# A transformer block, forward and backward: another order of all 1972 operations, other buffer homes, and one store that waits for a transpose

## The chip, the cores and the metric

The kernel runs on one core of a Trainium2 chip. The core has five engines, each with an instruction stream of its own: TensorE (PE, matrix multiplication; PEld is its loading of weights), VectorE (DVE), ScalarE (ACT), GpSimd (POOL) and SyncE (SP, which here only issues DMAs). They synchronise by semaphores. Operands lie in the SBUF (128 partitions), sums in the eight banks of the PSUM, and everything else in DRAM, from where and to where 16 DMA engines carry it. The metric is the time of one execution on the device in microseconds (us), the median of the runs; lower is better.

## What is computed

One block with pre-layer-norm, 2048 positions of 512 numbers in bfloat16: attention with 32 heads of 16, in which a position sees itself and seven earlier ones, two apart (a sliding window, dilated), and a dense pair of layers, 512 to 1792 to 512, with GELU between. The outputs are the block's result and its gradients for x and the weights and biases.

```
def _A_ref(x, wqkv, wo):
    ...
    off = jnp.arange(W) * dil            # W, dil = 8, 2
    idx = pos[:, None] - off[None, :]
    ...
    logits = jnp.einsum("bhsd,bhswd->bhsw", q, kg) * scale
    attn = _softmax(jnp.where(mask, logits, -1e9), axis=-1)
    o = jnp.einsum("bhsw,bhswd->bhsd", attn, vg)
    return merge_heads(o) @ wo

h  = x + _A_ref(_layernorm(x), A_wqkv, A_wo)
h2 = h + _B_ref(_layernorm(h), B_w1, B_b1, B_w2, B_b2)
...
_out, _vjp = jax.vjp(_f, A_x, A_wqkv, A_wo, B_w1, B_b1, B_w2, B_b2)
return (_out, *_vjp(grad_out))
```

(The lines are shortened; `merge_heads` stands for a transpose and a reshape.)

## The kernel before

The sequence is cut into four chunks of 512 rows, each of four tiles of 128 rows. The work of a chunk is written as stages, each a function that records operations: `p1_ln` to `p1_h` for the forward attention, `p2_h`, `p2_out`, `p2_dg` and `p2_bwd` for the dense layers and their backward pass, `p3_go` to `p3_gl1` for the backward pass of the attention, and `wg_ffn` for the gradients of the weights. An operation is a group of instructions on one engine with the buffers that it reads and writes. Nothing is issued while it is recorded. At the end of the function

```
    pl.emit(ORDER, HOMES)
```

issues all 1972 of them. `ORDER` is a table of their numbers: it sets the order of the program, and so the order on each engine and each queue. `HOMES` gives each buffer its place, in units of 64 bytes in the SBUF or as a PSUM bank. Two buffers may have the same place one after the other; the later one's writer then waits for the readers of the earlier one. `emit` requires that each operation stands behind those it depends on.

The table also decides a form of instruction. `mmul` (L268 and L270) writes a product with 128 weight columns either as one matmul (L270) or as four with 32 columns each (L268): the second form is taken in runs that stand between two operations which need 32 columns anyway (the sums L487 and L527).

What the steps of the prediction touch, in the order of a chunk's way through the kernel:

- `consts` and `warm` (L307 to L350) set constants at the start: `ident` by POOL, S (`S4`) by DVE from `ident`, `wz` by DVE, a block of zeros for fill matmuls on PE (L311).
- `layernorm` (L353 on): statistics st and mv by DVE (L360, L361), `ve` by DVE (L371), its power -1/2 `rstd` by POOL (L373), `nm` by DVE (L376), the scaled rows by ACT.
- `p1_attn`: the products `prf` of queries and shifted keys on DVE (L479), their sums on PE (L487), the largest `mx` on DVE (L690), its subtraction on PE (L270).
- `p1_o`: POOL gathers the neighbouring rows of v into R (L471, 2304 KB); DVE multiplies them with the coefficients to `prbo` (L518), four products for a chunk; PE sums each (L527); ACT puts the sum into `ost` (L532). Chunks 1 and 3 then get `ost` with rows and columns exchanged, `oT`, by a DMA transpose of SP (L291); the other two get it by PE. POOL stores `ost` to DRAM (L287, 512 KB) for the gradient of wo.
- `p1_h`: PE multiplies `oT` with wo, DVE adds x to h (L747), and the second layer norm follows.
- `p2_h`, `p2_dg`, `p2_bwd`: matmuls on PE with `w`, `w1T`, `w2T`, `goT` (transposed by SP, L291), evictions xb by ACT (L774), GELU gl by ACT (L777), its derivative by DVE and ACT (L792 to L803), gradients by DVE (L856), the layer norm backward (L561 to L570), which ends in `ghr`.
- `p3_go`: `ghT`, the transpose of `ghr` by SP (L291), times wo gives `got`, evicted by ACT (L297). `p3_dots` and `p3_bands` repeat the attention's kinds of products with the gathers Rq, Rk, Rv.
- `wg_ffn`: products over all rows for the gradients of the weights, evicted by ACT or DVE (L297) and stored (L287); the last are those of wqkv (`wgsq`).

The function that this change extends takes the buffers which an operation waits for as `r=`; so far a store waits for its source alone:

Of the kernel before, what the change touches and what calls it, by code (L numbers as in the profile page):

```python
# [159 lines left out]
def kernel(  # L160
# [30 lines left out]
    NC = S // CH  # L191
# [39 lines left out]
    ln2_t, o_t = ([dram.tile([P, TPC, D], BF16, name=f"{n}_d{c}") for c in range(NC)] for n in ("ln2", "o"))  # L231
# [12 lines left out]
    sb, ps_, op, fx = pl.sb, pl.ps, pl.op, pl.fixed  # L244
# [5 lines left out]
    ln1_d, ln2_d, o_d = ([fx(n, t) for t in ts] for n, ts in (("ln1", ln1_t), ("ln2", ln2_t), ("o", o_t)))  # L250
# [34 lines left out]
    def store(dst, ap, src, src_ap, kb, key=None, skey=None, q="SP", tag="store", row=1):  # L285
        e, us = (SY, 0.45) if q == "SP" else (A, 0.45) if q == "ACT" else (G, 0.6)
        return op(q, us, lambda: e.dma_start(out=ap(), in_=src_ap()), r=[(src, skey)], w=[(dst, key)] if dst is not None else (),  # L287
                  dma=kb / (DMA_RATE if row <= 1 else WIDE_RATE), tag=tag, piece=0.006 + 0.0385 * row, mode=5)
# [424 lines left out]
    def p1_o(c):  # L713
        d = st_[c]
        oT = d["oT"] = sb("oT%d" % c, [P, DC, CH])
# [10 lines left out]
        if c < ORR:  # L726
            store(o_d[c], lambda: o_t[c][:], ost, lambda: ost(), 512, q="POOL", tag="ost", row=4)
# [384 lines left out]
    for i in range(0 if W2PE else 4):  # L1112
        r = F // 4
# [222 lines left out]
```

## Time and profile before

| | us |
|---|---|
| median of 3 runs | 551.72 (551.65, 551.72, 554.88) |
| the profiled execution's own time | 553.64 |
| its span in the profile | 551.9 |
| PE busy in it | 538.8 |
| DVE busy | 494.2 |
| ACT busy | 324.2 |
| POOL busy | 25.8 |
| mean granted clock of PE | 0.997 |

The span runs from the first to the last recorded instruction; the execution's own time holds what lies around it as well. Busy times don't count the issuing of DMAs and the waiting. The rows of the views have the line of the kernel file, the engine, the operation, and out<-in by the names of the buffers, without the numbers that tell the chunks apart; "idle before" is the time in which an engine stood ahead of an instruction, and what is named behind `<-` is what let it go.

### The profile page before, as it was taken

Reading aid. Unit: us, or ns where it says so; the run is one execution under the profiler, and the core shown is the slowest. Engines: PE = TensorE matmul, PEld = TensorE weight load, DVE = VectorE, ACT = ScalarE, POOL = GpSimd, SP = SyncE. Lnnn points to the kernel's source line nnn. Section 1 sums busy time; section 2 is a strip of 40 time slices with the busy share of each in tenths; the row PEclk is TensorE's granted clock in tenths of the full one; section 3 lists DMA queues with packets and bytes.
Section 4 is the critical chain, followed back from the end, with each engine's and each line's share of the span. In section 5 each row is a group of like instructions: output and inputs, shape, how many; then the busy total and the mean of one; then the engine's idle time right before and its main releaser. Section 6 shows DMA issues by size and latency. Waiting matters only on the chain.

```text
span 551.9 us, 17462 instructions
## 1 busy us (share of the span) xinstructions
PE 538.8 (98%) x7764; PEld 286.7 (52%) x7764; DVE 494.2 (90%) x648; ACT 324.2 (59%) x507; POOL 25.8 (5%) x40
## 2 busy tenths in 40 slices
PE   7999999999989999999999999999999999999996
PEld 4756554444535445555555555465455555555542
DVE  7999999999979999999787089958899999999993
ACT  4987799989899876885341242034033376443521
POOL 1300100030001000000000000000010001000000
PEclk9999999999989999999999999999999999999999
DMA  8899998991597558679999999999999997888427
GB/s 279 226 291 281 417 302 190 201 332 83 74 235 251 137 98 197 201 121 214 197 191 219 182 194 192 291 218 281 213 279 425 335 338 284 355 290 187 128 60 190
DMA packets 195147, 126.68 MB, mean 230 GB/s; under 512 B 149760, under 2 KB 190656, under 8 KB 193024
## 3 DMA queue, kind: packets, MB, share of 16 engines
q1 hardware_dynamic: 189472, 81.79, 66.3%
q0 software_dynamic: 3408, 41.68, 19.8%
q10 hardware_dynamic: 2192, 2.10, 1.1%
q8 instruction: 60, 0.98, 0.8%
q14 instruction: 15, 0.12, 0.1%
HBM read 55.74 MB, written 35.21 MB: 165 GB/s over the span
## 4 chain that ended last, share of the span: by engine, by line
PE 55%; DVE 16%; ACT 4%; DMA 3%; issue 3%; SPq 2%; POOL 0%; ACTq 0%; DVEq 0%
PE ps L268 32%; PE ps L270 16%; PE ps L527 4%; DMA oT<-ost 2%; DVE xb L856 2%; DVE prbk L518 1%; DVE prbo L518 1%; DVE xb L803 1%; PE ps L487 1%; DVE prbv L518 1%; PE ps L543 1%; DVE x L799 1%; DVE st L360 1%; DVE h L747 1%; DVE h2s L828 1%
## 5 line engine op out<-in xcount | busy, mean ns | idle before, releaser
L479 DVE TENSOR_TENSOR prb<-got,vw 128x4096 bf16<-128x4096 bf16 x16 | 36.0, 2282 | 20.7 <-ACT got L297 13.8
L268 PE MATMUL ps<-w1T,xb 128*32 128x512 bf16 x896 | 53.1, 379 | 0.6 <-DVE h2s L828 0.4
L268 PE MATMUL ps<-goT,w2T 128*32 128x512 bf16 x832 | 50.5, 379 | 0.2 <-ACT xb L774 0.2
L297 ACT CAST wgs<-ps 128x512 bf16<-128x512 f32 (+1 forms) x30 | 16.2, 562 | 53.8 <-PE ps L270 30.4
L268 PE MATMUL ps<-w,gl 128*32 128x512 bf16 x776 | 46.3, 379 | 0.0
L856 DVE SCALAR_TENSOR_TENSOR xb<-xb,ps 128x512 bf16<-128x512 bf16 x56 | 36.9, 681 | 6.6 <-PE ps L268 6.4
L774 ACT ACTIVATE xb<-ps,b1c 128x512 bf16<-128x512 f32 x56 | 35.6, 703 | 10.1 <-PE ps L268 5.0
L268 PEld LDWEIGHTS <-xb 128*32 128x32 bf16 x896 | 26.2, 97 | 23.1 <-issue 1.2
L518 DVE TENSOR_TENSOR prbv<-Rv,cfv 128x4096 bf16<-128x4096 bf16 x16 | 35.7, 2284 | 1.4 <-PE ps L527 1.4
L518 DVE TENSOR_TENSOR prbq<-Rq,cfq 128x4096 bf16<-128x4096 bf16 x16 | 35.9, 2287 | 0.9 <-PE ps L270 0.4
L518 DVE TENSOR_TENSOR prbk<-Rk,cfk 128x4096 bf16<-128x4096 bf16 x16 | 35.9, 2284 | 0.3 <-PE ps L527 0.2
L518 DVE TENSOR_TENSOR prbo<-Ro,cfo 128x4096 bf16<-128x4096 bf16 x16 | 35.9, 2283 | 0.2
L479 DVE TENSOR_TENSOR prf<-qt,kt 128x4096 bf16<-128x4096 bf16 x16 | 35.7, 2283 | 0.0
L268 PEld LDWEIGHTS <-w2T 128*32 128x32 bf16 x832 | 24.0, 97 | 21.3 <-issue 0.5
L268 PEld LDWEIGHTS <-gl 128*32 128x32 bf16 x776 | 21.3, 97 | 21.1 <-ACT gl L777 1.3
L268 PE MATMUL ps<-wqkvT,gqkvT 128*32 128x512 bf16 x512 | 31.0, 379 | 0.0
L796 ACT ACTIVATE xb<-xb 128x2048 bf16<-128x2048 bf16 (+1 forms) x16 | 26.6, 1691 | 6.4 <-DVE xb L795 6.4
L626 PE MATMUL ps<-ln1T,wqk 128*32 128x512 bf16 x512 | 29.3, 381 | 0.7 <-ACT ln1T L297 0.7
L270 PE MATMUL ps<-ln2T,w 128*128 128x512 bf16 x120 | 27.4, 379 | 0.0
L792 ACT ACTIVATE x<-xb 128x2048 bf16<-128x2048 bf16 (+1 forms) x16 | 26.4, 1691 | 1.4 <-DVE h L747 1.3
L777 ACT ACTIVATE gl<-xb 128x2048 bf16<-128x2048 bf16 (+1 forms) x16 | 26.5, 1686 | 0.1
L561 ACT ACTIVATE gyr<-ps,rstd 128x512 bf16<-128x512 f32 x16 | 10.8, 677 | 23.5 <-PE ps L268 23.5
(199 smaller groups left out, 1085.7 us busy)
## 6 DMA issues: line engine op xcount, KB each, us to landing
Ro<-v_d POOLq DMA_DIRECT2D x4, 2304.0 KB, 11.6
Rq<-k_d POOLq DMA_DIRECT2D x4, 2304.0 KB, 11.5
Rv<-go_d POOLq DMA_DIRECT2D x4, 2304.0 KB, 13.9
Rk<-q_d POOLq DMA_DIRECT2D x4, 2304.0 KB, 14.1
g_d<-gl SPq DMA_DIRECT2D x9, 512.0 KB, 5.2
gh_d<-xb SPq DMA_DIRECT2D x9, 512.0 KB, 4.7
w<-in_B_w_dram SPq DMA_DIRECT2D x2, 1792.0 KB, 7.4
out_dram<-wgs SPq DMA_DIRECT2D x13, 256.0 KB, 4.7
```

What stands on the lines that cost most here:

```text
L268: T.matmul(out[32 * a:32 * a + 32, :], lhsT=l[:, 32 * a:32 * a + 32], rhs=r, start=start, stop=stop, skip_group_check=True)
L270: T.matmul(out, lhsT=l, rhs=r, start=start, stop=stop, skip_group_check=True)
L297: fn = lambda: A.copy(out=ap(), in_=pap())
L479: op("DVE", tt_us(4096), lambda g=g, pr=pr: V.tensor_tensor(out=pr(), in0=ql()[:, g, :].unsqueeze(1).to_broadcast([P, W, 512]), in1=_sub(k ...
L518: V.tensor_tensor(out=pr().rearrange("p a j (d h) -> p a j d h", h=H), in0=_sub(R()[:, o0, 0:1], [[st, 2], [512, 4], [32, DH], [1, H]]), i ...
L527: T.matmul(ps()[32 * j:32 * j + 32, :], lhsT=S4[:], rhs=pr()[:, hf, j, :], start=(hf == 0), stop=(hf == 1), skip_group_check=True)
L626: T.matmul(ps()[32 * a:32 * a + 32, gg * 512:(gg + 1) * 512], lhsT=_sub(wq_()[:, dc, 0:1], [[DH, H]], sel * D + 4 * g + a), rhs=rhs, start ...
L774: op("ACT", act_us(512, 1), lambda f=f, ps=ps, xb=xb, f0=f0: A.activation(out=xb()[:, f - f0, :], in_=ps(), func=ACT.Identity, bias=b1c[:, ...
L777: op("ACT", act_us(N), lambda xb=xb, gl=gl: A.activation(out=fl(gl), in_=fl(xb), func=ACT.Gelu_apprx_tanh), r=[xb], w=[gl], tag="gelu", mo ...
L792: op("ACT", act_us(N), lambda xb=xb, x2=x2: A.activation(out=fl(x2), in_=fl(xb), func=ACT.Square), r=[xb], w=[x2], tag="x2")
L796: op("ACT", act_us(N), lambda xb=xb: A.activation(out=fl(xb), in_=fl(xb), func=ACT.Tanh, scale=GC), w=[xb], tag="tanh", mode=6)
L856: op("DVE", 0.61, lambda f=f, ps=ps, z=z, f0=f0: V.scalar_tensor_tensor(out=z()[:, f - f0, :], in0=z()[:, f - f0, :], scalar=1.0, in1=ps() ...
```

## The change

Three things. A store may name further buffers that it waits for, and the store of `ost` of the last chunk (the fourth, which has its `oT` by DMA) now names `oT`: it is issued only after the transpose of its tile has been written. All other stores are as before.

```
-    def store(dst, ap, src, src_ap, kb, key=None, skey=None, q="SP", tag="store", row=1):
+    def store(dst, ap, src, src_ap, kb, key=None, skey=None, q="SP", tag="store", row=1, more=()):
...
-        return op(q, us, lambda: e.dma_start(out=ap(), in_=src_ap()), r=[(src, skey)], w=[(dst, key)] if dst is not None else (),
+        return op(q, us, lambda: e.dma_start(out=ap(), in_=src_ap()), r=[(src, skey)] + list(more), w=[(dst, key)] if dst is not None else (),
...
-            store(o_d[c], lambda: o_t[c][:], ost, lambda: ost(), 512, q="POOL", tag="ost", row=4)
+            store(o_d[c], lambda: o_t[c][:], ost, lambda: ost(), 512, q="POOL", tag="ost", row=4, more=[oT] if c == NC - 1 and c in FMO else ())
...
 ORDER = (
-    8, 10, 22, 7, 21, 12, 11, 0, 15, 9, 19, 1, 20, 16, 27, 17, 48, 6, 28, 14, 49, 50, 26, 51, 44, 25, 52, 29, 61, 45, 2, 24, 3, 46, 47, 53, 62, 136,
+    8, 0, 22, 12, 10, 1, 2, 15, 9, 21, 17, 18, 65, 6, 16, 7, 48, 27, 26, 11, 14, 49, 50, 28, 51, 52, 25, 3, 40, 29, 53, 4, 24, 5, 44, 41, 61, 139, 45,
...
 HOMES = (
...
```

`ORDER` and `HOMES` are new from the first row to the last; the same 1972 operations are issued. By the new neighbours 28 products with 128 columns become four matmuls with 32 columns each, and PE passes from one form to the other 28 times instead of 34, of these 12 instead of 16 after the place that is reached at 128 us in the trace of before.

What moves, at the places that matter below. The rows give the line, the operation, out<-in and the shape; the numbers behind a name tell buffers of one name apart and differ between the kernels.

At the start, DVE's first rows, before:

```order
L345 TENSOR_REDUCE S<-ident 128x32
L326 MEMSET epsc 128x1
L325 MEMSET mhalf 128x4
L307 MEMSET wz_2_106 128x256
L360 BN_STATS st<-xt_0_1_95 128x6
```

and now:

```order
L307 MEMSET wz_2_97 128x256
L326 MEMSET epsc 128x1
L345 TENSOR_REDUCE S<-ident 128x32
L654 MEMSET kt_12_4_122 128x4x8
L360 BN_STATS st<-xt_0_1_95 128x6
```

The block of zeros for the fill matmuls moves from behind the reduction of `ident`, which POOL makes, to the front.

DVE again, where the third layer norm of the first kind (its `ve` and `nm`) meets the first products `prf`, before:

```order
L371 TENSOR_SCALAR ve<-mv 128x4
L479 TENSOR_TENSOR prf_15_376<-qt_67_12_285,kt_86_13_358 128x4096
L376 SCALAR_TENSOR_TENSOR nm<-mv,rstd 128x4
L479 TENSOR_TENSOR prf_15_399<-qt_67_12_285,kt_86_13_358 128x4096
L479 TENSOR_TENSOR prf_18_446<-qt_67_12_285,kt_86_13_358 128x4096
```

and now:

```order
L371 TENSOR_SCALAR ve<-mv 128x4
L479 TENSOR_TENSOR prf_13_377<-qt_64_12_253,kt_12_4_122 128x4096
L479 TENSOR_TENSOR prf_15_403<-qt_64_12_253,kt_12_4_122 128x4096
L479 TENSOR_TENSOR prf_19_461<-qt_64_12_253,kt_12_4_122 128x4096
L658 COPY kt_122_20_484<-kt_12_4_122 128x4x16
L479 TENSOR_TENSOR prf_20_503<-qt_64_12_253,kt_12_4_122 128x4096
L479 TENSOR_TENSOR prf_19_562<-qt_127_21_521,kt_122_20_484 128x4096
L376 SCALAR_TENSOR_TENSOR nm<-mv,rstd 128x4
```

Between `ve` and the `nm` that needs POOL's power of it stand five products instead of one. In a later layer norm of the second kind the way is the other one: between `ve` and `nm` stand L755 and L793 before, and now L755 alone.

On SP's queue around the transpose `oT` of the last chunk (`ost` there is the tile that the changed store writes out, w1T are transposes of weights), before:

```order
L287 DMA out_dram<-h2s_32_1902 128x1x512 x3
L291 DMA_TRANSPOSE w1T_40_2249<-in_B_w_dram 128x14x128
L291 DMA_TRANSPOSE oT_600_40_2300<-ost_40_2158 128x16x128
L291 DMA_TRANSPOSE w1T_40_2249<-in_B_w_dram 128x14x128
L1079 DMA k_d<-zrow 16x512
```

and now:

```order
L287 DMA g_d_73<-gl_29_1794 128x4x512
L291 DMA_TRANSPOSE oT_599_38_2443<-ost_40_2281 128x16x128
L291 DMA_TRANSPOSE w1T_40_2499<-in_B_w_dram 128x14x128
L287 DMA out_dram<-h2s_35_2034 128x1x512
L291 DMA_TRANSPOSE w1T_40_2499<-in_B_w_dram 128x14x128
```

The transpose of weights ahead of `oT` is gone from there. On PE, between the last product sum of that chunk (L527) and the first matmul of wo with this `oT`, stand 160 matmuls of 32 columns before (32 + 32 + 48 + 48) and 224 now (32 + 48 + 48 + 32 + 16 + 48).

POOL's queue from the stores of the last two chunks to the first gather of the backward pass (`o_d` are the stores of `ost`, o_d_72 that of the last chunk), before:

```order
L287 DMA o_d_70<-ost_38_1770 128x2048
L471 DMA Ro_32_1965<-v_d 128x9216
L373 TENSOR_TENSOR rstd<-ve,mhalf 128x4
L287 DMA o_d_72<-ost_40_2158 128x2048
L373 TENSOR_TENSOR rstd<-ve,mhalf 128x4
L471 DMA Rq_46_6511<-k_d 128x9216
```

and now:

```order
L287 DMA o_d_71<-ost_33_1458 128x2048
L287 DMA o_d_70<-ost_34_1889 128x2048
L287 DMA o_d_72<-ost_40_2281 128x2048
L373 TENSOR_TENSOR rstd<-ve,mhalf 128x4
L471 DMA Rq_44_6589<-k_d 128x9216
```

Behind the store that now waits stands the power of the last layer norm as before, and then the gathers of the backward pass. In the rest of that part of POOL's queue the store of gq (`gq_d`) moves from ahead of the third gather of k (Rq) behind it.

At the end of the program PE's last products (`wgsq`) are followed by one eviction on ACT and a store of 128 KB; before, by two evictions and a store of 256 KB.

204 rows, old and new, of tables (HOMES, ORDER) are left out of this document.

## The prediction

> **What bounds the kernel now.** I read the page's busy shares and slices first, then what TensorE (PE) waits for, then the stretches around its longest wait. Busy times by engine and three rows of slices (40 slices of 13.8 us, tenths busy; PEclk is the granted clock):
>
> ```profile
> PE 538.8 (98%) x7764; PEld 286.7 (52%) x7764; DVE 494.2 (90%) x648; ACT 324.2 (59%) x507; POOL 25.8 (5%) x40
> PE   7999999999989999999999999999999999999996
> DVE  7999999999979999999787089958899999999993
> ```
>
> PE is idle for only 13.1 us of a span of 551.9, so no order can win more than that, what a lower clock costs, and what cheaper forms of matmul save. The view of waits names where the idle time lies (line waited at, releaser, total us, times, longest):
>
> ```profile
> PE ps L311 <- DVE wz L307: 2.0, 1, 2.0
> PE ps L268 <- DMA oT<-ost: 2.0, 1, 2.0
> PE ps L270 <- DVE mx L690: 1.2, 1, 1.2
> PE ps L268 <- DVE h2s L828: 0.4, 1, 0.4
> ```
>
> The first is the start, the second the wait for the transposed tile that the change also speaks of. Busy time by stretch (start:end, us, PE, PEld, DVE, ACT, POOL, clock, DMA share, GB/s):
>
> ```profile
> 0.00:106.00 106.00, 100.64 (x1289) 59.10 (x1293) 101.34 (x118) 88.45 (x115) 10.20 (x17) 1.00 0.93 276
> 140.00:180.00 40.00, 38.03 (x672) 19.19 (x668) 36.62 (x65) 36.97 (x39) 2.07 (x2) 0.96 0.84 193
> 300.00:340.00 40.00, 40.00 (x733) 22.02 (x722) 24.80 (x23) 12.09 (x23) 0.00 (x0) 1.00 1.11 193
> ...
> 156.00:158.00 2.00, 2.00 (x24) 0.85 (x28) 0.92 (x6) 2.00 (x2) 0.00 (x0) 0.58 0.80 174
> 158.00:160.00 2.00, 2.00 (x24) 0.79 (x20) 0.69 (x2) 2.00 (x2) 0.00 (x0) 0.57 1.21 236
> ```
>
> In the first 106 us VectorE (DVE) and PE are both nearly full, and DVE sets the pace: it is idle 106 - 101.34 = 4.7 us, with waits for ident, x and a power of GpSimd among them (rows below). From 140 on PE sets it, and by 300 DVE has 15 us in 40 to spare. After the 1.96 us wait near 155 the granted clock is 0.58 and 0.57 for two stretches of 2 us; PE lost (0.42 + 0.43) x 2 = 1.70 us there, so that wait cost 3.66 in all.
>
> **The change part by part.** I went through the new order engine by engine with the durations of the trace of before. Every term is a difference in span.
>
> *The transposed tile of the last chunk.* Its place in time order (start, us, engine and line, idle time before in brackets; SPq is SyncE's queue):
>
> ```profile
> 143.87 1.51 SPq L291 DMA_TRANSPOSE w1T<-in_B_w_dram  x1
> 144.70 0.62 PE L527 MATMUL ps<-prbo,S 128*32 128x512 bf16 x8
> 145.99 3.40 SPq L291 DMA_TRANSPOSE oT<-ost  x1
> 146.26 0.59 POOL L287 DMA_DIRECT2D o_d<-ost  x1 [22.34 <-ACT ost L532]
> ...
> 151.18 2.80 PE L268 MATMUL ps<-goT,w2T 128*32 128x512 bf16 x48
> 155.94 4.46 PE L268 MATMUL ps<-wo,oT 128*32 128x512 bf16 x48 [1.96 <-DMA oT<-ost]
> ```
>
> The transpose was issued at 145.99 and released PE at 155.94, 9.9 us later, with a transpose of weights issued 2.1 us ahead of it and the GpSimd (POOL) store of the same tile 0.3 us behind it. In the new order PE has 224 instead of 160 matmuls of 32 columns between the last product sum of this chunk and the first wo matmul: 64 x 2.80/48 = 3.7 us more cover, against a wait of 1.96. Even with the old landing the wait goes. No transpose of weights stands directly ahead any more, and the store now starts after the landing, so the landing should come sooner as well; that is worth nothing once the wait is gone. Bounds: 0 (the transpose lands 3.7 us later than before, or PE is short of other work) and -3.66. I take -1.96 and -1.70, nearer the second, since the cover alone is nearly twice the wait.
>
> [...]
>
> *The store's new wait.* POOL's queue holds behind that store only the power for the last layer norm and then gathers some 190 us later. The store itself takes 0.59. A wait of about 10 us there delays nobody unless it delays that power; bounds 0 and +0.5, I take 0. What covers it is that the power's input is made after the transposed tile has been used.
>
> *The start and the first part.* The beginning, and the power that DVE waited for:
>
> ```profile
> 1.33 0.29 DVE L345 TENSOR_REDUCE S<-ident 128x32 bf16<-128x128 bf16 x1 [1.33 <-POOL ident masks.py:199]
> 1.64 0.27 DVE L307 MEMSET wz<- 128x256 uint32 x1
> 1.97 4.37 PE L311 MATMUL ps<-wz 128*128 128x512 bf16 x10 [1.97 <-DVE wz L307]
> 2.85 0.69 DVE L360 BATCH_NORM_STATS2 st<-xt 128x6 f32<-128x512 bf16 x1 [0.93 <-DMA xt<-in_A_x_dram]
> 12.17 1.03 POOL L373 TENSOR_TENSOR rstd<-ve,mhalf 128x4 f32<-128x4 f32 x1 [10.72 <-DVE ve L371]
> 18.74 2.29 DVE L479 TENSOR_TENSOR prf<-qt,kt 128x4096 bf16<-128x4096 bf16 x1
> 18.88 3.02 POOL L373 TENSOR_TENSOR rstd<-ve,mhalf 128x4 f32<-128x4 f32 x1 [0.80 <-DVE ve L371]
> 21.93 0.26 DVE L376 SCALAR_TENSOR_TENSOR nm<-mv,rstd 128x4 f32<-128x4 f32 x1 [0.90 <-POOL rstd L373]
> 110.85 1.93 POOL L373 TENSOR_TENSOR rstd<-ve,mhalf 128x4 f32<-128x4 f32 x1 [22.58 <-DVE ve L371]
> 111.80 0.69 DVE L793 TENSOR_SCALAR ga<-x 128x2048 bf16<-128x2048 bf16 x1
> 112.81 0.16 DVE L376 SCALAR_TENSOR_TENSOR nm<-mv,rstd 128x4 f32<-128x4 f32 x1 [0.33 <-POOL rstd L373]
> ```
>
> The memset of wz moves to the front of DVE, so PE begins about 1 us earlier, but with fill matmuls: DVE still waits for x until 2.85, so this is 0 by itself. What counts is DVE's work ahead of each product against PE's ahead of its sum. Added up over the rows, DVE's greatest lead with its waits was 5.0 us (of the 5.4 that PE idled in the first 106 us); in the new order it is 4.3, at the sums of the last chunk: -0.7. The nm that waited 0.90 stands behind five products instead of one: -0.90. Another nm, at 112.81, loses the 0.69 at 111.80 from ahead of it while its power still takes up to 1.93: +0.6. Together -1.0. Bounds: 0 (DVE's lead stays) and -1.6 (no new wait for a power). Nearer the second, since the lead comes from counted rows.
>
> [...] That power took 3.02 beside a product of 2.29, against 1.03 beside statistics: it ended 0.87 after the product did, as if it had done its work only then. [...]
>
> *Form of the matmuls.* A run of 128-column matmuls beside runs of 32-column ones pays at each switch; the two rows after a switch and without one, and the groups of both forms:
>
> ```profile
> 441.79 1.83 PE ps L270 x8
> 461.96 1.73 PE ps L270 x8
> L268 PE MATMUL ps<-w,gl 128*32 128x512 bf16 x776 | 46.3, 379 | 0.0
> ```
>
> A switch costs 0.10. From 128 us on the order has 12 switches instead of 16: -0.4. 28 matmuls turn into four of 32 columns each: 4 x 46.3/776 = 0.239 against 1.73/8 = 0.216, so +0.6 at most, 0 if the mean holds the switches. I take +0.2 of that, together -0.2.
>
> *The end.* PE's last block is now followed by one eviction and a 128 KB store, before by two and 256 KB:
>
> ```profile
> 541.12 6.21 PE L270 MATMUL ps<-gks,ln1b 128*128 128x512 bf16 x28
> 546.91 1.07 ACT L297 CAST wgsq<-ps 128x512 bf16<-128x512 f32 x2 [1.07 <-PE ps L270]
> ```
>
> PE ends at 547.33, 4.6 before the span does. Half of 1.07 goes, less a little for what overlapped: -0.4, between 0 and -0.5.
>
> *New small waits from 129 to 310.* DVE is 3.4 us idle in 140 to 180, of which 1.08 + 1.31 in the two slow stretches, and ScalarE (ACT) 3.0. If PE comes 3.66 us earlier through that part, neither has much reserve, and by the rows several evictions and operands become tight. Bounds: 0 and +3.66 (DVE gives nothing back). I take +0.7, near the first, since DVE's reserve grows again soon after.
>
> Sum: -1.96 - 1.70 - 1.0 - 0.2 - 0.4 + 0.7 = -4.56, span 547.3. The profiled execution of before took 553.64, 1.74 more than its span, and the median of the runs is 551.72, 1.92 below that execution. So the new profiled execution would take 549.1 and the median 547.1.
>
> **The rivals.**
>
> *No new waits.* If the +0.7 does not come, the lost cover at 112.81 costs nothing (0.6), and the old small waits after 106 (0.4 for h2s and shorter ones, 1.2 together) vanish too (13.1 idle in all, less 5.4, 1.96 and 4.6 at the end): 547.1 - 0.7 - 0.6 - 1.2 = 544.6. For it: a whole new order can close small holes. Against: none is plainly covered by the rows.
>
> *A late transfer takes the place of oT.* Near 365 the last four blocks from a transposed ghT:
>
> ```profile
> DMA to landing us min/median/max: 4.5/5.3/6.2
> 361.73 3.12 SPq L291 DMA_TRANSPOSE ghT<-ghr  x1
> 371.17 1.89 PE L270 MATMUL ps<-ghT,woT 128*128 128x512 bf16 x8
> 363.89 2.29 DVE L479 TENSOR_TENSOR prb<-got,vw 128x4096 bf16<-128x4096 bf16 x1 [6.05 <-PE ps L487]
> ```
>
> Cover between issue and use was 9.4; in the new order it shrinks to about 6.6 from the work that makes ghr, against a longest landing of 6.2. If it lands as late as oT did (9.9), PE waits about 2 and the clock falls again: 547.1 + 2.0 + 1.7 = 550.8.
>
> *The power still holds DVE.* It does its 0.87 between two products wherever nm stands, and DVE's next product begins that much later: 547.1 + 0.9 = 548.0. For it: 3.02 beside a product. Against: PE's own lead may cover it. [...]
>
> *The lower clock does not hang on the wait for oT.* Then only the 1.96 goes, and the 1.70 is lost here or elsewhere: 547.1 + 1.7 = 548.8. For it: in the first 106 us PE waited 1.2 for mx and the clock of that stretch is 1.00. Against: the fall began at the very end of the longer wait. [...]
>
> *The change does not do what it says.* oT still lands too late, since PE reaches it sooner: 547.1 + 3.66 = 550.8.
>
> *Slower: gathers collide.* The late products wait for gathers issued on POOL in order:
>
> ```profile
> Rq<-k_d POOLq DMA_DIRECT2D x4, 2304.0 KB, 11.5
> Rk<-q_d POOLq DMA_DIRECT2D x4, 2304.0 KB, 14.1
> ```
>
> If two of them share their bandwidth with another twice, each lands 11.5 later, 23 in all, and DVE has the 6.05 of the row above in hand: 547.1 + 23 - 6.05 = 564.0. It decides from 6.05 + 4.6 + 5.5 = 16.2 us of delay on; one collision costs 5.5 and stays within 1%. For it: the store of gq moves behind a gather in POOL's queue. Against: the gathers' places in that queue are nearly the old ones.
>
> **How the numbers follow.** A difference under about 1% (546.2 to 557.2) is what a measurement of this kernel cannot well tell from none. Chances: forecast 0.47, with its own range 545.6 to 549; no new waits 0.15; a late transfer 0.13; the power 0.10; the clock 0.05; oT still late 0.04; gathers collide 0.06. Faster by over 1%: all of the second case and two fifths of the first, 0.15 + 0.19 = 0.34. Slower: 0.06. Same: 0.60. The range goes from 544.3 (the case without new waits, with the last of DVE's small ones gone) to 551.5 (the late transfer, 0.7 worse): outside lie the 0.06 above and about 0.12 at the two edges.
>
> **What would show it.** Right: no wait for oT in the view of waits and a clock of 1.00 between 140 and 180; PE's first matmul near 1.0; no DVE wait for a power near 22; a last eviction of one block. Wrong: a wait over 1 us for ghT, a gather or gelu with a clock under 0.9 behind it; DVE over 38 us busy in 40 between 140 and 180 with PE under 39; or PE busy above 540.

## The result, and the profile after

| | kernel before | changed kernel |
|---|---|---|
| median, us | 552.56 (551.65 to 554.88) | 571.3 (569.39 to 586.33) |
| the profiled execution's own time | 553.64 | 572.76 |
| its span | 551.9 | 571.0 |

The changed kernel takes 1.033 times as long, 95% interval 1.0305 to 1.0361: slower by 3.3%, where 547.1 was forecast and 0.06 was given to slower. The ratio leaves out executions more than 1.5% above a kernel's fastest, so the one of 586.33 is not in it; such executions turned out to be part of the answer and are told of below.

The busy times and slices of the changed kernel, from its page; the third row is the granted clock in tenths:

```profile
PE 542.7 (95%) x7848; PEld 291.0 (51%) x7848; DVE 494.4 (87%) x648; ACT 324.4 (57%) x507; POOL 25.9 (5%) x40
PE   8959999999999999999999999699989999999996
PEclk9987999999999999999999999799999999999998
```

The engines do what they did. PE is idle 28.3 us instead of 13.1, and the slices show where: the third (5) and the 26th (6), with a lower clock in the fourth and the 26th (7). The waits of PE name it:

```profile
PE ps L702 <- ACT e L697: 6.6, 1, 6.6
PE ps L270 <- DMA gw2in<-g_d: 5.0, 1, 5.0
PE ps L270 <- DMA gw1in<-gh_d: 2.3, 1, 2.3
PE ps L311 <- DVE epsc L326: 1.2, 1, 1.2
```

The wait for oT is gone, as forecast, and so are those for mx and h2s. Three larger ones stand elsewhere. The stretches around the two longest (columns as in the prediction; the clock is the first value behind POOL's):

```profile
36.00:43.00 7.00, 0.39 (x3) 0.11 (x2) 2.36 (x2) 2.42 (x3) 0.00 (x0) 0.69 0.79 292
43.00:49.00 6.00, 6.00 (x48) 2.52 (x51) 4.85 (x6) 5.43 (x7) 0.00 (x0) 0.51 0.25 87
...
357.00:362.00 5.00, 0.26 (x2) 0.00 (x0) 4.85 (x6) 0.45 (x1) 0.00 (x0) 0.75 1.05 191
362.00:366.00 4.00, 3.72 (x9) 1.34 (x10) 0.17 (x1) 0.00 (x0) 0.00 (x0) 0.50 1.23 302
```

Behind each of these two PE runs at half clock: it loses 6.00 x 0.49 = 2.9 us after the first and 3.72 x 0.50 = 1.9 after the second. Only the part of a slow spell in which PE works counts: the clock was already down while PE still stood (0.50 from 39 to 43 us and from 360 to 362), and that cost nothing. So the three waits with their slow spells take 6.6 + 2.9 + 5.0 + 1.9 + 2.3 = 18.7 us, nearly the 19.1 between the two spans; smaller new waits and a later end pay for what was won. This is the account of one profile; what the waits are worth in the time is the matter of the experiments.

**The first wait: a place in the SBUF that a store still reads.** PE waits for the exponential e, and e for what? The rows on POOL, SP, ACT and PE from 29 to 43 us, and the chain of waits over the same stretch:

```profile
29.49 0.74 POOL L471 DMA_DIRECT2D Ro<-v_d  x1 [7.29 <-PE ps L487]
...
30.43 1.45 SPq L287 DMA_DIRECT2D ln_d<-ln  x1
...
40.57 1.28 ACT L697 ACT_TABLE_LOAD   x1 [7.81 <-DMA ln_d<-ln]
41.87 1.02 ACT L697 ACTIVATE e<-ps 128x1024 bf16<-128x1024 f32 x1
...
42.94 1.01 PE L702 MATMUL ps<-e,ident 128*128 128x128 bf16 x8 [6.61 <-ACT e L697]
```

```profile
30.43 9.98 DMA ln_d<-ln
```

The new homes put e of the first chunk (unit 787 of the SBUF table) where the scaled rows ln of the third chunk had been. Those rows were being stored to DRAM, and the store, issued 0.9 us behind the first gather of v, took 9.98 us to land. ACT wrote e only after that: the store landed at 40.41, and ACT went on at 40.57. ACT's wait of 7.81 is for a transfer that only reads the place.

**The second wait: a transpose behind a gather.** The same kind of rows at 349 to 362 us:

```profile
349.14 0.60 POOL L471 DMA_DIRECT2D Rq<-k_d  x1 [156.00 <-PE ps L487]
350.31 1.54 SPq L291 DMA_TRANSPOSE gw2in<-g_d  x1
...
362.28 4.02 PE L270 MATMUL ps<-gor,gw2in 128*128 128x512 bf16 x9 [5.02 <-DMA gw2in<-g_d]
```

gw2in was issued 1.2 us behind a gather of 2304 KB and landed 11.9 us later; its median landing in this profile is 5.8. (Two other transposes stood in SP's issue from 343.74 to 350.25, just ahead of it; no run tells their part from the gather's.) The kernel before has such a transpose too: issued 1.3 us behind the second gather of its backward pass, it stood in SP's issue for 9.74 us, where the median for tmgod is 3.05:

```profile
379.60 0.53 POOL L471 DMA_DIRECT2D Rv<-go_d  x1 [26.81 <-DVE prbq L518]
380.88 9.74 SPq L291 DMA_TRANSPOSE tmgod<-got  x1
```

There nothing that PE needed next was among the transfers held up for 9.74 us.

**The store's wait does not exist.** The changed store and the transpose that it should wait for:

```profile
155.16 2.04 SPq L291 DMA_TRANSPOSE oT<-ost  x1
155.43 0.76 POOL L287 DMA_DIRECT2D o_d<-ost  x1 [19.66 <-ACT ost L532]
```

POOL issued the store 0.27 us behind the transpose's issue, and what let it go was the last eviction into ost. The list that the store now extends by oT says which operations must stand ahead of it in the table; `emit` only asserts this order (and that no two live buffers share a place) and then issues the same `dma_start`, which does not read oT. So by the code the argument changes no instruction, and the rows show no wait for oT. What was said of this wait ahead of the prediction, and its term there, is therefore wrong; the change is a new order and new homes.

### The profile page after: what moved, and what is told of

Its sections match the earlier page's. It is cut to its first block, busy times and chain, and to the rows that moved or that the text cites. A ratio compares the mean times of both kernels' runs of the same rounds, so it can differ in the third digit from the quotient of the medians.

```text
span 571.0 us, 17649 instructions
## 1 busy us (share of the span) xinstructions
PE 542.7 (95%) x7848; PEld 291.0 (51%) x7848; DVE 494.4 (87%) x648; ACT 324.4 (57%) x507; POOL 25.9 (5%) x40
## 4 chain that ended last, share of the span: by engine, by line
PE 59%; DVE 14%; issue 11%; DMA 9%; ACT 3%; SPq 2%; POOL 1%; DVEq 0%; ACTq 0%; POOLq 0%
PE ps L268 35%; PE ps L270 15%; PE ps L626 4%; PE ps L527 3%; DVE prbv L518 3%; DMA gw1in<-gh_d 2%; DMA gw2in<-g_d 2%; DMA ln_d<-ln 2%; DVE prbk L518 2%; DVE xb L856 2%; PE ps L487 1%; SPq L291 1%; DVE st L360 1%; DMA xw2in<-gl 1%; DVE h L747 1%
## 5 line engine op out<-in xcount | busy, mean ns | idle before, releaser
L268 PEld LDWEIGHTS <-xb 128*32 128x32 bf16 x896 | 26.3, 97 | 22.1
L268 PEld LDWEIGHTS <-gl 128*32 128x32 bf16 x792 | 23.2, 97 | 20.1 <-ACT gl L777 0.8
L268 PE MATMUL ps<-ln2T,w 128*32 128x512 bf16 x544 | 32.3, 379 | 0.3 <-DVE r L707 0.3
L626 PE MATMUL ps<-ln1T,wqk 128*32 128x512 bf16 x512 | 30.8, 389 | 0.7 <-ACT ln1T L297 0.7
L268 PE MATMUL ps<-gor,gw2in 128*32 128x512 bf16 x496 | 29.3, 379 | 0.3 <-DVE xb L856 0.3
L564 DVE CUSTOM_DVE_ANT_0 jk<-gyr,ln 128x512 bf16<-128x512 bf16 x16 | 10.9, 686 | 17.7 <-ACT gyr L561 12.1
## 6 DMA issues: line engine op xcount, KB each, us to landing
Rq<-k_d POOLq DMA_DIRECT2D x4, 2304.0 KB, 11.6
Rk<-q_d POOLq DMA_DIRECT2D x4, 2304.0 KB, 11.8
```

The lines of the kernel that those rows point to most:

```text
L268: T.matmul(out[32 * a:32 * a + 32, :], lhsT=l[:, 32 * a:32 * a + 32], rhs=r, start=start, stop=stop, skip_group_check=True)
L626: T.matmul(ps()[32 * a:32 * a + 32, gg * 512:(gg + 1) * 512], lhsT=_sub(wq_()[:, dc, 0:1], [[DH, H]], sel * D + 4 * g + a), rhs=rhs, start ...
```

## The experiments

Twelve kernels. Each time is the median with the range; the ratio is to the kernel before on the same chip, with its 95% interval, worked out as above. The kernels were timed on two chips (e2 and e6 to e8 on one, the others on the other); the medians of the kernel before on them, 552.04 to 552.36, differ by 0.1% at most.

| kernel | median (range), us | ratio |
|---|---|---|
| e1: changed, store without the new argument | 583.17 (570.74 to 590.05) | - |
| e2: before, store with the new argument | 552.13 (550.93 to 554.21) | 0.9993 (0.9973 to 1.0013) |
| e3: changed, store of ln first | 585.72 (581.26 to 599.21) | 1.0589 (1.053 to 1.0647) |
| e4: changed, e in another place | 567.86 (559.94 to 576.24) | 1.0187 (1.014 to 1.0233) |
| e5: changed, gw2in first | 571.1 (565.72 to 581.57) | 1.0318 (1.0258 to 1.0378) |
| e7: changed, transpose behind the gather | 570.46 (569.64 to 571.09) | 1.0318 (1.0285 to 1.0351) |
| e8: changed, transpose ahead of the gather | 593.92 (593.32 to 594.97) | 1.0745 (1.0711 to 1.078) |
| e6: four mended | 558.79 (554.1 to 569.39) | 1.0076 (1.0043 to 1.0108) |
| e9: e7, PE's wait filled | 571.38 (563.32 to 598.84) | 1.027 (1.0211 to 1.0329) |
| e10: e7, e in another place | 562.34 (558.75 to 564.42) | 1.017 (1.0134 to 1.0206) |
| e11: e7, gw2in first | 570.03 (566.65 to 580.25) | 1.0303 (1.026 to 1.0345) |
| e12: mended further | 559.68 (556.68 to 589.05) | 1.0118 (1.0074 to 1.0161) |

**The store's argument, e1 and e2.**

```
e1, against the changed kernel:
-            store(..., tag="ost", row=4, more=[oT] if c == NC - 1 and c in FMO else ())
+            store(..., tag="ost", row=4)
e2, against the kernel before: the same two lines the other way round, and the argument in store
```

> The changed kernel with its new order and homes, but the store of ost of the last chunk waits for its source alone again. Theory A (the order and the homes put three transfers that PE needs behind or beside 2304 KB gathers): the time stays at 569 to 573 us, with the same waits of PE of about 6.6, 5.0 and 2.3 us. Theory B (the store's wait upsets POOL's queue or the transposes and so costs most of it): the time falls below 560.

> The kernel before with its old order and homes, and with only the new wait: the store of ost of the last chunk waits for the transpose of its tile. Theory A: POOL has nothing due behind that store for 30 us, so the time is that of before, 550.5 to 553; if the store running beside the transpose had slowed the transpose, the 1.96 us wait for oT shrinks and up to 3.7 us are gained, 548 to 551. Theory B (the wait harms): over 555.

e2 takes as long as before (0.9973 to 1.0013), and e1 does not fall below 569: theory B is out. Since the argument changes no instruction, both are controls. In e1's profile the three waits of theory A are 5.1, 5.6 and 1.1 us. e1 is a second set of four executions of the changed program, and its 570.74, 580.59, 585.75 and 590.05 stand beside 569.39, 569.84, 572.76 and 586.33: this program has a spread of 21 us. Its profile differs from the first one above all at one place, where PE stood 5.7 us at 407 us and DVE 14.4 us. The view names no releaser there, but the second gather of the backward pass (Rv), which DVE needs, landed 26.2 us after its issue, just then:

```profile
393.69 5.79 SPq L291 DMA_TRANSPOSE tmgod<-got  x1
394.00 0.54 POOL L471 DMA_DIRECT2D Rv<-go_d  x1 [45.38 <-DVE prbq L518]
420.31 4.49 DVE L518 TENSOR_TENSOR prbv<-Rv,cfv 128x4096 bf16<-128x4096 bf16 x2 [14.42 <-issue]
```

That became theory E below. e2 is a second profile of the program before, and it says something about the forecast's first term, further down.

**The place of e, and the store that holds it, e3 and e4.** Numbers of operations: 292 is the store of ln, 293 the transpose of the same rows. In e4 one home changes, 787 to 3031 (buffer 61, e of the first chunk).

```
e3  ORDER:  ... 292, 293, ...        (292 stood eleven places behind 293)
e4  HOMES:  787  ->  3031
```

> The changed kernel, in which the store of the scaled rows ln of the third layer norm is issued on SP ahead of the transpose of the same rows, about 4 us before the first gather of v instead of 1 us behind it. The exponential e lies in the place of ln and so waits for that store. Theory A: the store lands before the exponential is due, the 6.6 us wait of PE near 36 us and the 10.2 us at half clock behind it (5.1 us lost) go, 559 to 564 us. Rival C (the exponential is late for another reason, such as its own operands or ACT's queue): nothing changes, 569 to 573.

> The changed kernel with one number of the homes changed: the exponential e of the first chunk lies in a place that nothing has used before, so it waits for no store. Everything else, the order too, is as in the changed kernel, and the store of ln is still issued behind the gather. Theory A: the same gain as with the store issued first, 559 to 564 us, and the store still lands about 10 us after its issue. If the late store itself held up PE in another way, the time would stay at 569 to 573.

e4: PE's wait for e is gone, at the same order. e3 is a miss that teaches more. Its store was early enough, but it pushed the transpose next to the gather, 2.7 us ahead of it and with its issue still running (4.78 us) when the gather began:

```profile
25.71 0.42 SPq L287 DMA_DIRECT2D ln_d<-ln  x1
26.17 4.78 SPq L291 DMA_TRANSPOSE ln1T<-ln  x1
28.90 0.74 POOL L471 DMA_DIRECT2D Ro<-v_d  x1 [6.67 <-DMA v_d<-tmv]
...
37.78 1.89 PE L270 MATMUL ps<-wv,ln1T 128*128 128x512 bf16 x4 [6.10 <-DMA ln1T<-ln]
40.60 1.28 ACT L697 ACT_TABLE_LOAD   x1 [7.48 <-PE ps L270]
```

PE waits 6.10 for ln1T instead of 6.61 for e. Neither the rival of e3 (another cause for e) nor the gain of theory A came true: in the profile the wait was passed to the next transfer beside the gather. (The collision at Rv stands in e3's profile too, with a wait of DVE of 11.8.) (The slow spells were put too high in both texts: half of 10.2 us counts the part in which PE stood as well.)

**A transpose on either side of a gather, e7 and e8.** 1499 is the transpose tmgod of the last chunk, 1270 the gather Rv, 1868, 1768 and 1754 are stores on SP.

```
changed:  ... 1868, ... 1768, ... 1499, ... 1270, ... 1754, ...
e7:       ... 1868, ... 1768, ...           1270, ... 1754, 1499, ...
e8:       ...                     1499, 1868, 1768, ... 1270, ... 1754, ...
```

> The changed kernel with one transpose on SP (tmgod from got of the last chunk) moved behind one more store, about 0.5 us later. In the profiles so far the second gather of the backward pass (Rv) was in DVE's hands 12 us after its issue where this transpose was issued behind it (0.2 us in the changed kernel, 1.6 in another), and 24 to 26 us after where it was issued 0.3 us ahead of it. Theory E (the order of these two decides, and in the changed kernel it is a matter of chance): now the transpose always comes second, the times lie within 568 to 573 in every run, and none is at 580 or more. Rival F (the spread has another cause, such as the clock): runs over 580 appear as before.

> The changed kernel with the same transpose on SP moved ahead of two stores, so that it is issued about 0.3 us ahead of the gather. Theory E: now the transpose always comes first, DVE waits 10 to 14 us for the gather in every run, and the times are 580 to 592 throughout. Rival F: the times spread between 569 and 586 as those of the changed kernel.

e7 came out as theory E says; e8 went the way it says and further (DVE waits 22.5 us instead of 10 to 14, and all times lie over 593). The runs of each agree within 0.3%: 570.46 and 593.92, 23.5 us apart. That is not the price of the two issues alone, since e8 puts two stores behind the transpose too, and e7 sets it behind a third; the one program of the changed kernel and e1 has 572.76 and 585.75 in its two profiled executions, 13.0 us apart, with the transpose 0.15 us behind the gather and 0.31 ahead of it. The issues and the first product that uses the gather, in the changed kernel, e7 and e8 in turn:

```profile
393.82 0.54 POOL L471 DMA_DIRECT2D Rv<-go_d  x1 [44.08 <-DVE prbq L518]
393.97 10.39 SPq L291 DMA_TRANSPOSE tmgod<-got  x1
```

```profile
394.03 0.53 POOL L471 DMA_DIRECT2D Rv<-go_d  x1 [44.04 <-DVE prbq L518]
394.43 9.12 SPq L291 DMA_TRANSPOSE tmgod<-got  x1
405.87 4.49 DVE L518 TENSOR_TENSOR prbv<-Rv,cfv 128x4096 bf16<-128x4096 bf16 x2
```

```profile
394.12 2.06 SPq L291 DMA_TRANSPOSE tmgod<-got  x1
394.45 0.54 POOL L471 DMA_DIRECT2D Rv<-go_d  x1 [43.99 <-DVE prbq L518]
428.87 4.49 DVE L518 TENSOR_TENSOR prbv<-Rv,cfv 128x4096 bf16<-128x4096 bf16 x2 [22.52 <-DMA out_dram<-wgs]
```

With the gather first, the transpose stands 9.12 us in SP's issue and the gather is used 11.8 us after its own. With the transpose first, SP is free after 2.06, and the gather is used 34.4 us after its issue. The last row names a store of wgs: e8 moved this store behind the transpose, and the product's place lies over the store's source. The store landed 1.2 us behind the gather, which itself took 33.1; the transpose took 33.7. The last value of a stretch's row is what the DMA engines moved, in GB/s; the changed kernel, then e8:

```profile
394.00:398.00 4.00, 4.00 (x74) 1.86 (x76) 4.00 (x3) 0.65 (x2) 0.36 (x1) 1.00 1.05 330
398.00:402.00 4.00, 4.00 (x80) 2.00 (x76) 4.00 (x3) 1.08 (x2) 0.00 (x0) 1.00 0.98 359
```

```profile
400.00:404.00 4.00, 4.00 (x82) 1.94 (x74) 3.98 (x2) 0.12 (x1) 0.00 (x0) 1.00 0.88 83
416.00:420.00 4.00, 0.00 (x0) 0.00 (x0) 0.00 (x0) 0.00 (x0) 0.00 (x0) 0.50 1.43 91
420.00:424.00 4.00, 0.00 (x0) 0.00 (x0) 0.00 (x0) 0.00 (x0) 0.00 (x0) 0.50 1.21 50
```

From 394 to 402 us of the changed kernel, while the transpose stands in SP's issue, the engines move 330 and 359 GB/s. With the transpose ahead, transpose, gather and stores all crawl (33.7 and 33.1 us to land, a store of wgs 29.6): in the seven stretches of 4 us from 400 to 428 of e8 the engines are as busy (0.6 to 1.4) but move 50 to 129 GB/s, and PE, DVE and ACT do nothing in the two later stretches shown. In the changed kernel the two issues lay 0.15 us apart, so an execution could fall on either side, and that of e1 did. The late executions of e1, e3, e4 and e5 fit that: in the profiles of e1, e3 and e4 the transpose was issued 0.25 to 0.3 us ahead, and DVE waited 11.6 to 14.4 us; in that of e5 it was 1.5 us behind, and DVE did not wait for the gather. That each late time had this cause isn't shown, since only one execution of a kernel was profiled. Nor does e7's order rule late times out: e11 has it and one execution at 580.25 (in its profile the transpose was issued only 0.11 us behind the gather), and e12 has it and one at 589.05 (there 2.1 us behind), of which nothing is known.

**The transpose that PE waits for, e5 and e11.** 1755 is the gw2in transpose, 1247 and 1374 the transposes tmgod of two other chunks.

```
e5, e11:  ... 1755, 1247, ... 1374, ...      (1755 stood behind 1374)
```

> The changed kernel with one transpose of GELU rows (gw2in, the one PE waits 5.0 us for near 357 us) issued on SP two transposes earlier, about 6 us ahead of the first gather of k instead of 1 us behind it. Theory A: that wait and the 6.8 us at half clock behind it (3.4 us lost) go, 561 to 565 us; what was issued there before (the transposes of got) lands later instead and may give back 1 or 2. Rival D (the DMA engines are saturated near 350 us whatever the order): the wait moves to the next transpose of SP, and the time stays within 2 us of 571.

> The changed kernel with tmgod behind the gather, and the gw2in transpose two places earlier. This prices the second wait alone: 4.9 us of wait and 3.4 us at half clock go, at most 2.5 come back as waits for what was moved behind: 561.5 to 565.

The wait for gw2in is gone from both profiles, but neither kernel reached the time expected: both medians stay within 2 us of 571, as rival D said. e11's median is 0.4 us under e7's, and its five nearer times are 566.65 to 572.77. Its profile shows the gain partly handed on, as rival D has it too: DVE waits 2.8 for the next transpose (tmgod), and PE then 2.3 for a product of DVE (pp) near 356 us. So a price of this wait alone isn't shown, and rival D is not out.

**The place of e alone, e10.** e7 and the home of e4.

> The changed kernel with tmgod behind the gather, and the exponential e in a place of its own. Without the chance of the second gather this prices the first wait alone: 6.7 us of wait and 3.4 us for the half clock go, less what DVE's own work then limits: 560 to 564, and the runs within 4 us of each other.

The median is as expected: 570.46 - 562.34 = 8.1 us for one number of the table, against 6.6 + 2.9 = 9.5 in the profile; the ratios, 1.0318 and 1.017, say the same. (The six times lie 5.7 us apart, not 4.) Its store of ln was still issued behind the gather; nothing waited for it.

**Filling the wait, e9.**

```
         def esum():
+            if c == 0:
+                for _ in range(28):
+                    T.matmul(pss(), lhsT=ident[:], rhs=ident[:].unsqueeze(1).to_broadcast([P, 4, P]), start=True, stop=True, ...)
             for w in range(W):
```

> The changed kernel with tmgod behind the gather (as the run whose times were 569.6 to 571.1), and 28 matmuls more on PE just ahead of the first sums of the exponential e, whose results are overwritten: 28 x 0.216 = 6.0 us of work inside the 6.7 us wait. Theory G (the granted clock falls because PE idles there): the wait shrinks to under 1 us, the clock stays at 1.00 near 43 us, and although PE does more, the time falls by the 3.4 us that 6.8 us at half clock cost, 566 to 568. Rival H (the clock falls for another reason, or the lower clock costs nothing because DVE sets the pace there): the time stays at 569.5 to 571.5.

The clock part of theory G holds in the one profile: e7's stretch, then the same in e9:

```profile
43.00:49.00 6.00, 4.90 (x36) 2.15 (x39) 3.72 (x5) 5.99 (x9) 0.00 (x0) 0.50 0.26 89
```

```profile
36.00:44.00 8.00, 6.69 (x36) 3.11 (x35) 2.27 (x2) 2.67 (x3) 0.00 (x0) 1.00 0.68 256
44.00:50.00 6.00, 5.71 (x94) 3.07 (x95) 5.50 (x6) 6.00 (x8) 0.00 (x0) 1.00 0.27 90
```

The times don't confirm it (a median of 571.38 with a range of 35.5 us). In the profiled execution, the latest of them, other collisions stand: PE waits 9.6 us for gw2in, and a transpose goT was issued 0.45 us ahead of the last gather of the forward pass:

```profile
119.03 3.62 SPq L291 DMA_TRANSPOSE goT<-gor  x1
119.48 0.59 POOL L471 DMA_DIRECT2D Ro<-v_d  x1
...
150.62 1.87 PE L270 MATMUL ps<-goT,w2T 128*128 128x512 bf16 x4 [21.05 <-DMA goT<-gor]
```

PE went on 31.6 us after its issue, having stood 21.05. In the changed kernel's profile the gather came 1.6 us behind this transpose, in e7's 1.9, and nobody waited. That the fill alone moved the two queues against each other is likely, but not shown.

**The order without its collisions, e6 and e12.** e6 has the home of e4, the order of e5 and e7, and the transpose gw1in (1819) earlier on SP, into another place, with another gw1in (1821) later for it. e12 has the first three, and two other edits: ln1T ahead of the two stores that the first gather waits for, and three of the last stores (two of gx and, unlike what was expected of it, that of gbs) ahead of PE's last blocks.

> The changed kernel with its four late transfers mended together: the exponential e in a place of its own, the gw2in transpose two places earlier, the gw1in transpose (2.3 us of wait near 423 us) earlier by its own place and order, and tmgod behind the gather. Theory A: 11.7, 8.4 and 2.3 us go and up to 3 come back as other small waits, so 547 to 553, about the kernel before, and the runs agree within 2 us. If it stays over 558, the new order has further costs that these waits only covered.

> The changed kernel with e in its own place, gw2in earlier and tmgod behind the gather, and two things more: the transpose ln1T near 25 us ahead of the two stores that the first gather waits for, so that it has landed before that gather starts (its wait of 1.7 to 2.5 us near 31 us goes), and three of the last stores of gx ahead of the last blocks of PE (the 5.7 us behind PE's last matmul become 4.6). If the collisions are all that the new order costs: 550 to 554, as the kernel before. If the first gather then comes too late for DVE, a new wait of 2 to 4 us near 45 us takes it back.

e6 gives back most of the loss, 558.79, 1.0076 times the kernel before, but neither its expected time (547 to 553) nor runs within 2 us: they reach from 554.1 to 569.39, and its profiled execution (564.17) still has waits of 2.5 for ln1T and 2.2 for gw1in. Against e10, which it extends by gw2in and gw1in, it goes from 1.017 to 1.0076, some 5 us, where the profile of the changed kernel has 5.0 + 1.9 + 2.3 = 9.2 for these two. e12's profiled execution has a span of 554.9 and no wait of PE over 1.5 us; its longest:

```profile
PE ps L626 <- ACT ln1T L297: 1.4, 1, 1.4
PE ps L268 <- ACT got L297: 1.4, 1, 1.4
PE ps L311 <- DVE epsc L326: 1.2, 1, 1.2
PE ps L270 <- DMA gw1in<-gh_d: 1.1, 1, 1.1
```

The wait for ln1T at 31 us is gone in e12, and no wait of 2 to 4 us replaced it. But its times reach from 556.68 to 589.05, none in the expected 550 to 554, and its median is not below e6's. In its profile the span ends 5.4 us behind PE's last matmul, 5.8 in e6's, so the store edits moved little. Neither beats the kernel before, and no run points to a version of this order that would.

## Why the prediction was wrong

- **The wait for oT** (-1.96 and -1.70): the direction was right, the wait is absent from the changed kernel's profile, and the clock is 1.00 between 140 and 180 us. Its size was an accident of the profiled execution. The second profile of the same program (e2) has a span of 549.4 and this row:

```profile
PE ps L268 <- DMA oT<-ost: 0.6, 1, 0.6
```

  No slow spell follows it: no matmul of wo with oT took over 390 ns there, against up to 634 in the first profile. The prediction noted that the median lay 1.92 under the profiled execution and carried that over as a constant, though the stall itself may well make this difference. In e2's execution, nearer to the median, there were 0.6 us to win here, not 3.66. (551.72 - 4.56 is 547.2, not 547.1.)
- **The store's new wait** (0): free, but only because it does not exist. The rival "the change does not do what it says" looked for this at the transpose, not at the store.
- **The start and the first part** (-1.0): PE starts at 1.20 instead of 1.97. The nm that had waited 0.90 waits no more, and another one, at 121 us, waits 0.90 instead of 0.33, both as forecast. The rest was buried under the wait for e. The rival of a power that holds DVE fell: the power took 2.98 us beside three products, against 1.01 beside statistics at 15.75, but the products took 6.69 together, as three without it (6.68). So here POOL took longer and DVE did not.

```profile
19.05 6.69 DVE L479 TENSOR_TENSOR prf<-qt,kt 128x4096 bf16<-128x4096 bf16 x3
31.68 6.68 DVE L479 TENSOR_TENSOR prf<-qt,kt 128x4096 bf16<-128x4096 bf16 x3
19.22 2.98 POOL L373 TENSOR_TENSOR rstd<-ve,mhalf 128x4 f32<-128x4 f32 x1 [2.46 <-DVE ve L371]
```

- **The form of the matmuls** (-0.2): too small to be read from PE's busy times (538.8 and 542.7), which hold the slow spells as well.
- **The end** (-0.4): wrong sign. The span ends 5.7 us behind PE's last matmul, before 4.6. ACT's last store is smaller, but three stores of gx on SP came after it. The forecast looked at ACT's queue alone.
- **New small waits from 129 to 310** (+0.7): this is the step that failed. It weighed engines against engines, and only in this stretch; outside it the sum had no term for a new wait of PE. What came, at 36, 357 and 423 us, all outside, was 14 us of waits that transfers held up and 4.8 us of half clock behind them. Two omissions made it. A buffer's place was taken as free when the last engine had done with it, while a store was still reading it (e, worth 8.1 us in e10). And every transfer in the sum kept the landing time of before, wherever the new order put it relative to a gather; e6 against e10 gives some 5 us for mending gw2in and gw1in.
- **The rival "a late transfer takes the place of oT"** (0.13) had the kind of wait right and the transfer and the number wrong: ghT, which it named, held PE for 0.8 us, and gw2in, e's store and gw1in held it for 5.0, 6.6 and 2.3. Two of the signs of being wrong showed: a late transpose of GELU rows (gw2in) with a clock of 0.50 behind it, and PE busy for 542.7.
- **The rival "gathers collide"** had the right suspect and the wrong partner. It let two gathers share a bandwidth and needed 16.2 us of such delay; a single transpose issued 0.3 us ahead of one gather goes with 13.0 more in one program (e1's profile against the changed kernel's), and with 23.5 where stores stand behind it too (e8 against e7). Its 0.06 was low for a new order that had moved gathers and transposes against each other.
- **The clock.** Waits of 6.61 and 5.02 us were followed by a clock of 0.51 and 0.50, and one of 2.3 at 423 us was not followed by a fall (the stretch from 420 to 460 has a clock of 1.00). In the first profile one of 1.96 was followed by 0.58 and 0.57, and e2's of 0.6 by no slow spell. So these profiles don't show from which length of a wait on the clock falls: it fell behind the one of 1.96 and not behind the longer one of 2.3.

What stays open: 4 to 7 us between e6 or e12 and the kernel before (0.8 and 1.2%), of which the profiles show a later end (about 1) and several waits of 1 to 1.5, none of them tried by itself; the price of gw2in alone; why gw1in is late; the cause of e12's late execution; and what in the two queues makes the order of issue matter so much.

## What to carry to other kernels

When a search gives a new order, go through the transfers before the engines: for each wait that has to be met, what is issued on any queue within a few microseconds of a large gather (here 2304 KB, and from 2.7 us ahead of it to 1.2 behind), and which side of it. A buffer's place is free when the last transfer that reads it has landed, not when it was issued (here 9.98 us later). And compare two profiles, or the profiled time with the median, before a stall of 2 us in one execution is counted as something to win.

## What the runs showed of the hardware

- A DMA transpose on SP and a 2304 KB gather on POOL, issued within half a microsecond of each other: with the gather first, it was used 11.8 us after its issue (changed kernel, e7), and the engines moved 330 and 359 GB/s from 394 to 402 us of the changed kernel; with the transpose first, 23.5 to 26.3 us (e1, e3, e4) and 34.4 (e8, with stores behind the transpose), at 50 to 129 GB/s in e8's stretches from 400 to 428. Transposes issued first were late too: tmgod landed after 33.7 us in e8, and PE had goT 31.6 us after its issue in e9. Issued 1.6 us ahead of a gather, goT was used 10.6 us later and held nobody up (changed kernel).
- A plain store of ln, issued 0.9 us behind a gather, took 9.98 us to land in the changed kernel, whose gathers Ro took 9.7 to 15.6 and whose fastest store of ln 3.6. SP's next transpose behind a gather stood in its issue for 9.12 us in e7.
- The changed kernel and e1 are one program, whose two issues lie 0.15 and 0.31 us apart on either side in the two profiles. It took 569 to 573 us in four executions and 581 to 590 in four others.
